# One skip op, tied weight loads, last value sums first, and three opening exps on VectorE in a fused attention and state-space kernel

**Chip, cores, metric.** One core of one Trainium2 chip. The metric is the device time of one execution in microseconds (us), lower is better. Each version was run several times; the rounds ran on different chips, each with runs of the kernel before beside the others. A stage's length is read from one profiled execution. The profile's span ends some 2 us before the reported time.

## The reference, cut to what matters

```python
def reference(A_x, A_Lambda_re, ..., B_wqkv, B_wo, gate_w):   # x: 1 x 2048 x 1024, bf16
    g = sigmoid((x * gate_w).sum(-1))
    # A: a state-space layer, h[t] = Lam_bar * h[t-1] + x[t] @ B_bar.T
    #    y = 2 * Re(h @ C.T) + x * Dskip                 <- the "skip"
    # B: attention, 32 heads of 32 columns, softmax over 2048 keys, then @ wo
    return g * a + (1 - g) * b
```

## The kernel before

The attention is cut into 512 bursts: TensorE (PE) makes the scores of four heads by 256 queries by 256 keys, ScalarE (ACT) or VectorE (DVE) takes the exponentials, PE multiplies with the values. The state-space work is woven in as dense chains of matmuls. The first 16 bursts are the opening: they run while the projections of the first heads are still being made and while GpSimd (POOL) makes the products from which the tables of the scan are built. ACT takes all exps of 128x1024, except that in the bursts of the set `DVB` VectorE takes half of one tile in four steps:

```python
def dve_exp(self, B, s, p):
    ...
    self.S.op("act", lambda e: e.activation(t[:, 0, :], ps[:, 2 * s, :], ACT.Exp, ...), ...)
    # exp_a: PSUM -> SBUF, frees the score bank when it is done
    self.S.op("dve", lambda e: e.tensor_scalar(xi, ps[:, 2 * s + 1, :], BITS_0, BITS_MIN, ALU.add, ALU.max), ...)
    # exp_b, exp_c, exp_d: each with two inputs in SBUF
    self.dx += [(0.603, lambda: self.dve(lambda e: e.scalar_tensor_tensor(xw, lo, 65536.0, lo, ALU.subtract, ALU.mult), ...)),
                (0.603, lambda: self.dve(lambda e: e.scalar_tensor_tensor(xw, lo, CUBE_C, xw, ALU.add, ALU.mult), ...)),
                (0.603, lambda: self.dve(lambda e: e.scalar_tensor_tensor(bits, xw, CUBE_K, xi, ALU.mult, ALU.add), ...)), ...]
```

POOL's products in the opening, 128x1024 f32, four multiplications and two additions:

```python
def products():
    for n, (u, v) in enumerate(((0, 0), (1, 1), (0, 1), (1, 0))):
        self.pool(lambda e, n=n, u=u, v=v: e.tensor_tensor(pr[n], hi[u], lo[v], ALU.mult), ...)
        if n % 2:
            ...
            self.pool(lambda e, ...: e.tensor_tensor(out, pr[n - 1], pr[n], ALU.add if r else ALU.subtract), ...)
```

The end of the last burst, and the end of each engine's stream, where a flag made from the row sums decides whether a safe second version must run (it never does here):

```python
        self.pv([(last - 1, q) for q in range(4)])
        preload()      # four matmuls, sum of the other heads' output
        pv(0)          # last value sums, 2 x 8 matmuls
        norm(0)
        pv(1)
...
            S.emit(name, e, sems, MARK_AT[name], lambda: loc.append(e.mark_branch_hint_location()))
            ...
            e.wait_ge(sems[fast.flag_op.lane], fast.flag_op.tick)
            with e.register("bad_" + name) as r:
                e.reg_load(r, flag[0:1, 0:1])
                br = e.br_cmp(r, 0, on_true="done_" + name, on_false="bad_" + name, comp_op="IS_EQ")
                ...                        # the second version stands between the branch and "done"
```

Of the kernel before, what the change touches and what calls it, by code (L numbers as in the profile page):

```python
# [735 lines left out]
class GpPhaseA:  # L736
# [216 lines left out]
ORDER = "".join(w[0] * int(w[1:]) for w in (  # L953
    "u2 p3 u2 p1 u3 p3 u1 p7 u3 p1 u3 p5 u1 p1 u5 p1 u1 p3 u2 p1 u1 c3 p1 c1 p2 u1 p1 u2 p1 c2 p1 c1 p1 u2 p1 u1 p1 u1 p3 c1 u3 p5 c1 u1 p1 u3 c1 p4 u2 p1 "
    "c1 u2 p1 c2 u2 p8 u2 p1 c1 p1 u2 p1 c5 p1 c5 u4 p3 u2 p4 u2 p1 u2 p1 u2 p3 u2 p3 u1 p2 u1 p5 c8 p2 o36 ").split())
DVB_RUNS = ((70, 70), (73, 73), (78, 82), (90, 94), (97, 97), (108, 108), (114, 114), (117, 117), (122, 122), (125, 125), (130, 130), (138, 142), (145, 149), (155, 155), (158, 158), (161, 161), (166, 166), (171, 171), (174, 174), (179, 179), (182, 214), (217, 217), (222, 226), (229, 229), (234, 250), (253, 253), (258, 262), (265, 265), (270, 274), (277, 277), (282, 290), (293, 305), (308, 308), (314, 318), (321, 321), (324, 324), (329, 329), (332, 332), (338, 342), (347, 347), (350, 354), (365, 365), (370, 370), (373, 373), (382, 382), (385, 389), (394, 394), (397, 397), (406, 410), (413, 417), (420, 420), (426, 426), (429, 429), (434, 438), (441, 445), (450, 450), (453, 453), (459, 459), (462, 470), (473, 481), (486, 490), (493, 497), (502, 506))
DVB = {B for lo, hi in DVB_RUNS for B in range(lo, hi + 1, 4)}
REST = 508
FIRST = 16
# [23 lines left out]
class FastPath:  # L983

    def __init__(self, nc, S, es, d, flag):
# [32 lines left out]
        self.prow = T("prow", [40, 128], BF)  # L1018
        self.pf = T("pf", [128, 40, 8], F32)
        self.W = T("W", [128, 2, 2, 8], F32)  # L1020
# [3 lines left out]
        self.drow = T("drow", [128, 1024], BF)  # L1024
        xa = T("xa", [128, 256], BF)
        self.init = T("init", [128, 2, 8], F32)
# [5 lines left out]
        self.badb = T("badb", [128, 2], BF)  # L1032
        self.xn = [xa[:], self.pf[:, 24:40, :].bitcast(BF).rearrange("p a b -> p (a b)")]

# [18 lines left out]
        self.xi = [wx[0][:, 2048:3072], wx[1][:, 2048:3072], self.ut[:, 0, :]]  # L1053
        self.xi = [ap.bitcast(F32) for ap in self.xi]
        self.xw = [ag, ag, self.ut[:, 1, :]]
        self.tile += self.xt
# [22 lines left out]
    def act(self, fn, r, w, name=""):  # L1079
        return self.S.op("act", fn, reads=r, writes=w, name=name)  # L1080

# [13 lines left out]
    def ld_w(self, g, part, eng="sp"):  # L1095
        cb = 1024 * part + 128 * g
        deps = []
        for t in self.x_toks(g % 2) if g > 2 else []:
            deps += [self.S.tok_w.get(t)] + list(self.S.tok_r.get(t, []))
        self.S.op(eng, lambda e: e.dma_start(self.w[:, g % 2, part], self.wsrc[:, :, cb:cb + 128]), writes=[("w", g % 2, part)], deps=deps, name="ld_w", dma=True)  # L1100
# [79 lines left out]
    def opening(self):  # L1180
# [12 lines left out]
        for word in self.OPENING.split():  # L1193
# [11 lines left out]
            elif op == "Kb":  # L1205
                self.half256(1, i, 1)
                evac(self.K[:, 0, 256 * i:256 * (i + 1)], 7, ("K", 0, i // 2), i % 2 == 0)
                self.spare(SPARE_K[i])
            elif op == "Qb":
                self.half256(0, i, 1)  # L1210
                evac(self.Q[:, i // 2, 256 * (i % 2):256 * (i % 2 + 1)], 7, ("Q", i // 2), i % 2 == 0)
                self.spare(SPARE_Q[i])
            elif op in ("Va", "Vb"):
# [8 lines left out]
                if h:  # L1222
                    src = ps[:, bank, 0:258].rearrange("p (k c) -> p k c", k=2)
                    S.op("dve", lambda e, i=i, src=src: e.tensor_copy(self.V[:, 0, 2 * i:2 * i + 2, :, 0:32], src[:, :, 0:128].rearrange("p k (h c) -> p k h c", h=4)),
                         reads=[("bank", bank)], name="evac_v", **(dict(acc=[("V", 0, i // 2)]) if i % 2 else dict(writes=[("V", 0, i // 2)])))
                    dve(lambda e, i=i, src=src: e.tensor_copy(self.gcol[:, 0, 2 * i:2 * i + 2], src[:, :, 128]), [("bank", bank)], [("g0", i)])
                    self.spare(SPARE_V[i])
            elif op == "G":
# [5 lines left out]
            elif op == "B":  # L1234
                self.burst(8 * U + i)()
                while self.later and self.later[0][0] <= self.p:
                    self.later.pop(0)[1]()
                self.p += 1
            elif op == "M":
                S.op("pe", lambda e: e.matmul(ps[:, 6, 0:40], self.prow[:], self.ident[0:40, 0:40], start=True, stop=True),  # L1240
                     reads=[("prm", i) for i in range(5)] + ["ident"], writes=[("bank", 6)], name="prm")
                dve(lambda e: e.tensor_copy(self.pf[:, 0:5, :], ps[:, 6, 0:40].rearrange("p (a b) -> p a b", a=5)), [("bank", 6)],
                    [("pf", i) for i in range(5)], "prm")
                dve(lambda e: e.tensor_copy(self.wv0[:, :, 128], self.pf[:, 4, :]), [("pf", 4)], ["wv0g"])
                self.bg2, self.bg3 = self.math()
                self.nmath = len(self.bg2)

    def spare(self, us):
# [102 lines left out]
    def ld_xn(self, ch, tq, cb):  # L1351

        tt = 4 * ch + tq
        for k in range(2):
            over = ["iot", "ioth", "ioti"] + [("pw2", l) for l in range(4)] if k and self.c_next == 0 else []
            c0 = 512 * cb + 256 * k
            self.dma(lambda e, k=k, c0=c0: e.dma_start(self.xn[k], self.x2[128 * tt:128 * (tt + 1), c0:c0 + 256]), [], [("xn", k)] + over, "ld_xn")
        self.c_next += 1

    def skip_ops(self, ch, tq, cb):  # L1360

        tt = 4 * ch + tq
        ops = []
        for k in range(2):
            c0 = 512 * cb + 256 * k
            ops.append((0.335, lambda k=k, c0=c0: self.dve(lambda e: e.scalar_tensor_tensor(self.Ag[:, 0, 256 * k:256 * (k + 1)], self.xn[k], self.gcol[:, 0, tt:tt + 1],
                                                                                            self.drow[:, c0:c0 + 256], ALU.mult, ALU.mult),
                                                           [("xn", k), "drow", "g0"], [("Ag", 0), ("sc", 0)] if k == 0 else [("Ag", 0, 1)], "skip")))
        ops.append((0.0, lambda: self.c_next < 32 and self.ld_xn(*self.c_list[self.c_next])))
        return ops  # L1370
# [16 lines left out]
    def table_ops(self, j):  # L1387
# [10 lines left out]
        def op(c, fn, r, w, *late):  # L1398
            ops.append((c, lambda: self.dve(fn, r, w)) + late)
        op(0.27, lambda e: e.tensor_scalar(S[:, :, 0:128], bj[:, :, 0:128], w(1, 0), None, ALU.mult), b0 + self.EFtok, [sc] + (["m_a0", "m_a1", "m_a2", "m_k", "m_h", "m_y"] if j == 0 else []))  # L1400
        for r, alu in ((0, ALU.subtract), (1, ALU.add)):
# [135 lines left out]
    def d_c(self, ch, tq, cb, k):  # L1537
# [15 lines left out]
        def evac():  # L1553
            self.dve(lambda e: e.scalar_tensor_tensor(a, ps[:, 7, :], self.gcol[:, 0, tt:tt + 1], a, ALU.mult, ALU.add), [("bank", 7), "g0", ("Ag", 0, 1)], [at], "evac_c")  # L1554
            self.dma(lambda e: e.dma_start(self.agd[tile], a), [at, ("Ag", 0, 1)], [("agd", tile)], "st_a")
            self.c_left[ch] -= 1
            self.c_end = self.p
# [172 lines left out]
    def x_set(self, B):  # L1730
        return 2 if B >= 433 else self.x_group(B) % 2

# [50 lines left out]
    def dve_exp(self, B, s, p):  # L1783
# [6 lines left out]
        wg = self.x_group(B)  # L1790
        use = (k, wg if k < 2 else 0)
        self.x_now = k
        if use not in self.seen_x:
            self.seen_x.add(use)
            if k < 2:
                assert self.busy_w != wg and not self.proj[wg]
                over = [("w", k, q) for q in range(3)] + [("Ag", 1), "m_h", "m_y"]
            else:
# [82 lines left out]
    def build(self):  # L1881
# [7 lines left out]
        self.dx, self.seen_x, self.waiting, self.x_now, self.busy_w = [], set(), set(), None, None  # L1889
        self.bg2, self.bg3 = [], []  # L1890
        self.begin()
# [53 lines left out]
        log = self.log = []  # L1945
        self.dx_end = {}
        for p in range(first, NBURST):
# [55 lines left out]
            if g + 2 < GROUPS:  # L2003
                assert g or pg != 24 or not (proj[0] or cur and cur.tag == "proj")
                for k, part in enumerate((1, 2, 0)):
                    if pg == (58 + 2 * k if g else 24):
                        self.ld_w(g + 2, part)
# [141 lines left out]
    def tail(self):  # L2149
# [61 lines left out]
        self.pv([(last - 1, q) for q in range(4)])  # L2211
        preload()
        pv(0)
        norm(0)
        pv(1)
        xp(0)
# [137 lines left out]
```

## Time and profile before

| | before |
|---|---|
| time, median of 3 runs | 918.78 us (918.45 to 919.16) |
| span of the profiled run | 916.8 us |
| first exp starts | 9.77 us |
| first normalization of a head ends the opening | 49.23 us |
| last full normalization | 899.32 us |
| flag write starts | 914.08 us |

The last four rows cut the span into five stages: **start** (to the first exp), **opening** (to the first 128x8 reciprocal of a normalization), **middle** (to the last such reciprocal), **tail** (to the flag) and **end**. The lines that show what bounds each stage stand in the prediction.

The end of the opening, its rows in the timeline (start, duration, engine, line, operation, output <- inputs):

```profile
39.55 0.17 DVE L1231 TENSOR_SCALAR f_gcol<-f_gcol 128x16 f32<-128x16 f32 x1 [0.86 <-ACT f_gcol L1230]
...
42.50 0.68 DVE L1523 CAST f_ub<-f_ps 128x512 bf16<-128x512 f32 x1
42.64 0.37 PE L1853 MATMUL f_ps<-f_V,f_OT 128*128 128x33 bf16 x8
...
43.32 1.02 PE L1517 MATMUL f_ps<-f_xT,f_wb 128*128 128x512 bf16 x4
```

At 39.55 VectorE waits 0.86 us for ACT, whose queue holds the sigmoid of the gate; then it makes the gate's column `gcol`, and from 40.13 the tables of the scan. The cast is the first evacuation (copy out of PSUM) of a chain `u`, the product of x with the input matrix of the state-space layer; it stands behind the tables in VectorE's queue. PE's next chain, which needs the bank, starts at 43.32.

### The profile page before, as it was taken

The numbers are of one execution on the slowest core, as the hardware profiler recorded it, in microseconds if no ns is written. First come the engines' busy times: TensorE is split into PE (matmuls) and PEld (weight loads), VectorE is DVE, ScalarE is ACT, GpSimd is POOL, SyncE is SP. The second block draws the span as 40 slices with busy tenths as digits, with TensorE's granted clock in tenths as the row PEclk, the third lists the DMA queues.
The fourth block names the chain that finished last, engine by engine and source line by source line (L and its number), as shares of the span: only waits on it lengthen the run. The fifth ranks groups of instructions, "written<-read, shape, count | busy, mean of one in ns | idle before, by whom it ended". The sixth has DMA issues, their size and how long they took to land.

```text
span 916.8 us, 33709 instructions
## 1 busy us (share of the span) xinstructions
PE 902.4 (98%) x15196; PEld 513.6 (56%) x15196; DVE 757.3 (83%) x1394; ACT 902.1 (98%) x1034; POOL 33.4 (4%) x63
## 2 busy tenths in 40 slices
PE   8999999999999999999999999999999999999997
PEld 4556655555555655665556555556555655555554
DVE  4499998999989899998988975789999776676675
ACT  6999999999999999999999999999999999999997
POOL 0500000010000001000000010000000000000000
PEclk9999999999999999999999999999999999999999
DMA  9558631322311305222222113231330122533422
GB/s 205 108 88 129 105 59 40 54 44 57 87 39 39 72 24 86 44 51 48 62 65 31 49 62 87 66 63 31 54 63 8 52 65 70 177 88 119 123 65 75
DMA packets 166867, 65.37 MB, mean 71 GB/s; under 512 B 146880, under 2 KB 155584, under 8 KB 166720
## 3 DMA queue, kind: packets, MB, share of 16 engines
q1 hardware_dynamic: 164416, 62.52, 30.8%
q8 instruction: 120, 1.97, 0.9%
q10 hardware_dynamic: 2304, 0.67, 0.3%
q14 instruction: 27, 0.22, 0.1%
HBM read 21.24 MB, written 12.62 MB: 37 GB/s over the span
## 4 chain that ended last, share of the span: by engine, by line
PE 92%; DVE 3%; ACT 3%; DMA 1%; issue 0%; SPq 0%
PE f_ps L1853 26%; PE f_ps L1758 18%; PE f_ps L1545 12%; PE f_ps L1517 12%; PE f_ps L1485 11%; PE f_ps L1578 6%; PE f_ps L1505 5%; ACT f_cT_re L1781 1%; DVE f_tq L1423 1%; ACT f_pt L1781 1%; DMA f_xT<-in_A_x_dram 1%; ACT f_cT_im L1781 1%; ACT f_Et L1781 1%; ACT f_OT L1781 1%; DVE f_ht L1431 1%
## 5 line engine op out<-in xcount | busy, mean ns | idle before, releaser
L1781 ACT ACTIVATE f_pt<-f_ps 128x1024 bf16<-128x1024 f32 x840 | 800.5, 1156 | 1.2 <-PE f_ps L1758 0.6
L1853 PEld LDWEIGHTS f_ps<-f_V,f_pt 128*128 128x128 bf16 x6720 | 232.8, 96 | 137.1 <-issue 86.5
L1853 PE MATMUL f_ps<-f_V,f_pt 128*128 128x33 bf16 x6720 | 285.4, 178 | 0.3
L1758 PE MATMUL f_ps<-f_Q,f_K 32*128 32x256 bf16 x4096 | 213.1, 273 | 2.6 <-ACT f_cT_re L1781 1.2
L1758 PEld LDWEIGHTS f_ps<-f_Q,f_K 32*128 32x128 bf16 x4096 | 67.4, 92 | 120.9 <-ACT f_pt L1781 63.4
L1517 PE MATMUL f_ps<-f_xT,f_wb 128*128 128x512 bf16 x512 | 131.1, 377 | 1.5 <-DVE f_ub L1523 0.4
L1485 PE MATMUL f_ps<-f_xT,f_wb 128*128 128x512 bf16 x464 | 119.0, 378 | 0.3 <-DVE f_Q L1490 0.2
L1431 DVE TENSOR_TENSOR_SCAN f_ht<-f_pf,f_init,f_ut 128x512 bf16<-128x512 f32 x64 | 81.2, 1275 | 0.0
L1805 DVE TENSOR_SCALAR f_wb<-f_ps 128x512 f32<-128x512 f32 x83 | 56.8, 685 | 27.4 <-PE f_ps L1758 26.5
L1545 PE MATMUL f_ps<-f_cT_re,f_hp 128*128 128x512 bf16 x192 | 72.6, 378 | 0.9 <-DVE f_Ag L1554 0.8
L1545 PE MATMUL f_ps<-f_cT_im,f_hp 128*128 128x512 bf16 x192 | 72.5, 378 | 0.0
L1578 PE MATMUL f_ps<-f_wb,f_OT 128*128 128x512 bf16 x248 | 63.9, 378 | 0.2
L1804 ACT ACTIVATE f_wb<-f_ps 128x512 bf16<-128x512 f32 x83 | 60.8, 732 | 0.6 <-PE f_ps L1758 0.6
L1517 PEld LDWEIGHTS f_ps<-f_xT,f_wb 128*128 128x128 bf16 x512 | 40.3, 96 | 34.2 <-issue 2.2
L1505 PE MATMUL f_ps<-f_wb,f_xT 128*128 128x128 bf16 x896 | 59.1, 219 | 0.3
L1812 DVE SCALAR_TENSOR_TENSOR f_wb<-f_Ag,f_wb 128x512 int16<-128x512 f32 x83 | 56.7, 683 | 0.6
L1811 DVE SCALAR_TENSOR_TENSOR f_Ag<-f_wb,f_Ag 128x512 f32<-128x512 uint16 x83 | 56.7, 683 | 0.5
L1810 DVE SCALAR_TENSOR_TENSOR f_Ag<-f_wb 128x512 f32<-128x512 uint16 x83 | 56.6, 682 | 0.3
L1485 PEld LDWEIGHTS f_ps<-f_xT,f_wb 128*128 128x128 bf16 x464 | 36.2, 96 | 28.7 <-DVE f_Q L1490 0.3
L1505 PEld LDWEIGHTS f_ps<-f_wb,f_xT 128*128 128x128 bf16 x896 | 50.5, 97 | 0.9 <-issue 0.4
L1523 DVE CAST f_ub<-f_ps 128x512 bf16<-128x512 f32 x48 | 33.1, 690 | 14.8 <-PE f_ps L1517 14.1
L1423 DVE TENSOR_TENSOR f_tq<-f_ht,f_Et 128x1024 bf16<-128x1024 bf16 x64 | 42.8, 685 | 0.4
(158 smaller groups left out, 892.7 us busy)
## 6 DMA issues: line engine op xcount, KB each, us to landing
ag_scratch<-f_Ag SPq DMA_DIRECT2D x32, 256.0 KB, 2.0
f_hp<-ag_scratch SPq DMA_DIRECT2D x32, 256.0 KB, 3.0
f_wb<-in_B_wqkv_dram SPq DMA_DIRECT2D x21, 256.0 KB, 4.0
out_dram<-f_xT SPq DMA_DIRECT2D x14, 256.0 KB, 2.1
f_xa<-in_A_x_dram SPq DMA_DIRECT2D x32, 64.0 KB, 1.9
f_pf<-in_A_x_dram SPq DMA_DIRECT2D x32, 64.0 KB, 1.9
f_wb<-in_B_wo_dram SPq DMA_DIRECT2D x1, 1024.0 KB
f_OT<-f_On SPq DMA_TRANSPOSE x63, 2.3
```

What stands on the lines that cost most here:

```text
L1431: ops.append((1.192, lambda ri=ri: dve(lambda e: e.tensor_tensor_scan(ht[:, ri, :], rr, ut[:, ri, :], self.init[:, ri, j:j + 1], ALU.mult, ...
L1485: mms.append((1, lambda e, f, l, a=a: e.matmul(ps[:, bank, :], w[:, g % 2, part, a, :], xT[:, a, 512 * ch:512 * (ch + 1)], start=f, stop=l ...
L1505: m = e.matmul(ps[:, bank, 128 * q:128 * (q + 1)], xT[:, a, 128 * kt:128 * (kt + 1)], w[:, g % 2, 2, a, :], start=(a == 0), stop=(a == 7))
L1517: mms.append((1, lambda e, f, l, a=a: e.matmul(ps[:, 7, :], bT[:, n % 2, ri, a, :], xT[:, a, 512 * ch:512 * (ch + 1)], start=f, stop=l), [ ...
L1545: mms.append((1, lambda e, f, l, j=j, ri=ri: e.matmul(ps[:, 7, :], hp(tq, ri, j), cT[ri][:, j, 512 * cb:512 * (cb + 1)], start=f, stop=l), ...
L1578: mms.append((1, lambda e, f, l, j=j: e.matmul(ps[:, 7, :], OT[:, j, 256 * qb + 128 * r:256 * qb + 128 * (r + 1)], wo[j][0][:, 512 * cb:51 ...
L1758: m = e.matmul(ps[:, 2 * sl[z] + h % 2, 256 * kl:256 * (kl + 1)], K[32 * h:32 * h + 32, g % 2, 128 * kt:128 * (kt + 1)], Q[32 * h:32 * h + ...
L1781: self.act(lambda e: e.activation(self.tile[p], ps[:, 2 * s:2 * s + 2, :], ACT.Exp, bias=OCTAVES * LN2, scale=LN2 / 128), [("S", s)], [("p ...
L1804: self.S.op("act", lambda e: e.activation(t[:, 0, :], ps[:, 2 * s, :], ACT.Exp, bias=OCTAVES * LN2, scale=LN2 / 128), reads=[("S", s)], wr ...
L1805: self.S.op("dve", lambda e: e.tensor_scalar(xi, ps[:, 2 * s + 1, :], BITS_0, BITS_MIN, ALU.add, ALU.max), reads=[("S", s)], writes=[("xi" ...
L1811: (0.603, lambda: self.dve(lambda e: e.scalar_tensor_tensor(xw, lo, CUBE_C, xw, ALU.add, ALU.mult), [I, W], [W], "exp_c")),
L1853: m = e.matmul(ps[:, 6, o:o + 33], self.tile[p][:, h2, 256 * kl + 128 * qt:256 * kl + 128 * (qt + 1)], V[:, g % 2, 2 * i + kl, h, :], star ...
```

## The change

The intent: give ACT less to do in the opening and at the very end, shorten the last serial chain, and use fewer, larger instructions for the skip. Weight loads are tied to an exp, and 24 tiny memsets, the pads, stand ahead of VectorE's stream; the record doesn't say what the pads are for. Core of the diff (cuts marked):

```diff
-DVB_RUNS = ((70, 70), (73, 73), ... (502, 506))
+DVB_RUNS = ((7, 7), (12, 12), (14, 14), (70, 70), (73, 73), ... (502, 506), (509, 509))
 ...                                   # and small exchanges in ORDER, the order of dense work
-        self.xi = [ap.bitcast(F32) for ap in self.xi]
+        self.xi = [ap.bitcast(F32) for ap in self.xi] + [self.Ag[:, 0, :]]   # scratch in the state bank
-        for k in range(2):            # x for the skip: two loads of 128x256
-            self.dma(... self.xn[k], self.x2[..., c0:c0 + 256] ...)
+        self.dma(... self.xn, self.x2[128 * tt:128 * (tt + 1), 512 * cb:512 * (cb + 1)] ...)
 ...                                   # one 128x512 skip op for two of 128x256
-        deps = []
-        for t in self.x_toks(g % 2) if g > 2 else []:
+        deps = [self.last_act] if g > 1 else []                              # tied weight loads
+        for t in self.x_toks(g % 2) if g > 1 else []:
+        for _ in range(24):
+            self.dve(lambda e: e.memset(self.chk[:, 5:6], 0.0), [], ["pad"])
-        preload()
         pv(0)
         norm(0)
+        preload()
         pv(1)
```

## The prediction

> **What bounds the kernel now.** I read the page first, then the stretches of five to ten microseconds, then the timeline of the first 56 and the last 20 us, last the chain of waits. The page's first part has two engines full at once and VectorE (DVE) behind them:
>
> ```profile
> PE 902.4 (98%) x15196; PEld 513.6 (56%) x15196; DVE 757.3 (83%) x1394; ACT 902.1 (98%) x1034; POOL 33.4 (4%) x63
> ```
>
> PE and ACT are both at 98%, so an average names no bound; it has to be found per stage. The stretches (columns: us, then busy time and count of PE, PEld, DVE, ACT, POOL, then clock, DMA share, GB/s) do that:
>
> ```profile
> 25.00:30.00 5.00, 4.81 (x66) 3.24 (x64) 2.86 (x10) 5.00 (x6) 3.76 (x2) 1.00 1.16 175
> 30.00:35.00 5.00, 4.18 (x61) 2.94 (x60) 1.41 (x5) 5.00 (x7) 4.92 (x4) 1.00 0.80 173
> 35.00:40.00 5.00, 4.62 (x77) 3.08 (x72) 1.40 (x6) 5.00 (x7) 3.64 (x2) 1.00 0.02 5
> 50.00:60.00 10.00, 10.00 (x197) 5.73 (x190) 9.91 (x18) 10.00 (x12) 0.71 (x1) 1.00 0.53 89
> ```
>
> In the opening (16 bursts, first exp at 9.77 us, last ends near 41 us) ACT is never idle, while PE has gaps and DVE is two thirds idle from 30 to 40 us: ACT bounds it. From 50 us on PE and ACT are both full, and until 100 us DVE too. Note POOL: it is at work from 26 to 39 us and nearly nowhere else. The last burst is a serial chain of PE, DVE and ACT.
>
> [...]
>
> ```profile
> 190.95 2.12 POOL L1456 TENSOR_TENSOR f_cm<-f_hl,f_W 128x8 f32<-128x8 f32 x4
> 191.12 0.68 DVE L1812 SCALAR_TENSOR_TENSOR f_wb<-f_Ag,f_wb 128x512 int16<-128x512 f32 x1
> 191.72 1.30 DVE L1423 TENSOR_TENSOR f_tq<-f_ht,f_Et 128x1024 bf16<-128x1024 bf16 x2
> ...
> 362.06 0.68 POOL L1456 TENSOR_TENSOR f_cm<-f_hl,f_W 128x8 f32<-128x8 f32 x4
> ```
>
> The same four POOL products take 0.68 us where DVE reads PSUM, and 2.12 us beside two-input DVE instructions, whose own length stays at 0.68. Here POOL waits, not DVE; a long POOL instruction against DVE is not in this trace. [...] The twelve warm-up matmuls take 4.46 us in the trace, the first ones 0.43 us apart[...]. [...]
>
> **The change, part by part.**
>
> *Three exps of the opening.* Bursts 7, 12 and 14 run as the 11th, 13th and 15th. ACT drops one 128x1024 exp in each to 128x512. Full exps: the 11th burst's starts at 28.22 us and the 16th's at 37.25, so ten take 9.03 us, 0.903 each. Half an exp is seen at the end (start, duration, engine):
>
> ```profile
> 898.71 0.79 ACT L1804 ACTIVATE f_ub<-f_ps 128x512 bf16<-128x512 f32 x1
> ...
> 899.18 8.56 ACT L1781 ACTIVATE f_pt<-f_ps 128x1024 bf16<-128x1024 f32 x9
> ```
>
> The next starts 0.47 us on. Saved: 0.903 - 0.47 = 0.43 each, 1.3 us for three. DVE gets four 128x512 instructions each at about 0.6 us start to start, 3 x 2.4 = 7.3 us, from 28 to 40 us, where its idle time is about 7 us: it fits just, and the evacuations slip by less than one burst.
>
> *One more at burst 509.* The ACT row above is back to back up to the last exp, so ACT bounds the last bursts too; a gain of up to 0.43, call it 0.35, as PE has only some 0.3 us of wait a burst there.
>
> *Last value sums first.* The end of the chain before:
>
> ```profile
> 909.01 0.55 PEld L2162 LDWEIGHTS f_ps<-f_Et,f_ident 128*128 128x128 bf16 x4
> 909.04 1.02 PE L2162 MATMUL f_ps<-f_Et,f_ident 128*128 128x512 bf16 x4
> 909.68 0.47 PEld L2173 LDWEIGHTS f_ps<-f_V,f_pt 128*128 128x128 bf16 x8
> 909.90 0.36 PE L2173 MATMUL f_ps<-f_V,f_pt 128*128 128x33 bf16 x8
> 910.29 0.18 DVE L2180 RECIPROCAL f_rc<-f_ps 128x4 f32<-128x4 f32 x1 [0.91 <-PE f_ps L2173]
> ```
>
> Four preload matmuls stand ahead of the eight value sums that the reciprocal waits for. Exchanged, the sums start at about 909.1, the reciprocal near 909.55, and the preload fills PE while DVE normalizes (0.76 us of PE wait there before). The second sums then wait for the preload's end, near 910.3 instead of 911.02. Gain about 0.7.
>
> *24 pads.* The new DVE program starts with 24 one-column memsets, each waiting for the one before, ahead of the memset that releases the warm-up. The warm-up before ends at 5.71 us (1.25 + 4.46), the first projection starts at 6.67, when its transposed load has landed; 0.96 us is free. A DVE accumulator read (one column) takes 0.08 us, so I estimate 0.08 per pad, 1.9 us in all: the projection starts near 7.6, 0.95 late. A second load wait of 0.16 us is absorbed: cost 0.8 us, moved straight into the first exp, as nothing in the opening has slack on ACT. At 0.04 us a pad it would be nothing, at 0.12 it would be 1.8.
>
> *Skip op, weight loads, order of work.* Two 128x256 skip instructions start 0.39 us apart, 0.79 a pair; one of 512 columns should take about 0.66 (256 more columns at 0.96 per ns). 32 x 0.13 = 4 us of DVE, in a stage where DVE has idle time: 0 on the path. One 128 KB load for two of 64 KB: hidden. Group 2's weights come 34 bursts later and all others are tied to an exp; they land within 4 us and are first needed about six bursts on, some 10 us: 0. Two small exchanges in the order of dense work: 0, give or take 0.5.
>
> *Sum without a new wait:* -1.3 - 0.35 - 0.7 + 0.8 = -1.55, or 917.2 us.
>
> **The rivals.** (1) *POOL's products become the wait.* The tables' first DVE instruction needs POOL's last product:
>
> ```profile
> 36.36 2.36 POOL L1323 TENSOR_TENSOR f_OT<-f_hp 128x1024 f32<-128x1024 f32 x1
> ...
> 40.13 0.35 DVE L1400 TENSOR_SCALAR f_Ag<-f_OT,f_rc 128x256 f32<-128x256 f32 x1
> ```
>
> POOL ends at 38.72, DVE comes at 40.13: 1.4 us of slack, which a shorter opening uses up. POOL reads SBUF all the while, and of the nine new two-input DVE instructions (three per exp) about eight fall beside it. If each holds POOL off for 0.53 us (512 columns at 0.96 per ns), POOL ends 4 us later, and DVE, which works in order, stands before the tables for some 3 us with the first u evacuation behind them; PE's next chain needs that bank, and PE works in order too. That would swallow the opening's gain and add about 3 us: 920 to 922. For it speaks the pair of POOL rows above; against it, that these were tiny instructions[...]. If instead the long POOL instruction (1.9 to 2.4 us) holds DVE off, exp_a of the next burst comes late, score banks stay taken and ACT stalls: 923 to 925. Against that: no two-input DVE row in the trace is longer than its kind. (2) *The pads dominate:* 0.12 us each gives +1.8, about 918.3. (3) *Nothing carries:* PE takes over as the bound in the last six opening bursts (it is busy 4.2 to 4.8 of 5 us) and only half of 1.3 us is seen: 917.9.
>
> I give the case without a new wait six in ten, the POOL wait three, DVE held off by POOL one. That weights the point by +0.4: 917.6 us. The range takes half of the POOL cases: 915.5 to 921.3. A gain of 2% would be 18 us; everything touched is below 10 us, so faster 0.01, same 0.98, slower 0.01.
>
> **What would show it.** Right: the first exp at about 10.6 us instead of 9.77, ACT without gap until the 16th burst's end near 40.4, three 128x512 exps there, POOL's end before 40 us, the first sums' reciprocal less than 0.6 us after the last score matmuls' sums, and 50 to 890 us as long as before. Wrong: POOL products longer than 1.91 and 2.36 us, a DVE wait of microseconds ahead of the tables, with PE idle near 44 us; or a first projection at 6.7 us (pads free) or after 8.5 (pads dear). If the middle stage (100 to 890 us) moves by more than 1 us, the order of work mattered, and my zero there is the failed step.

Two things that the prediction uses are seen in the traces with these numbers. The column rate: in the kernel before, VectorE's casts out of PSUM took 690 ns for 128x512 and 424 for 128x256, so 256 more columns took 266 ns, 0.96 per ns; the 0.66 us for a skip op and the 0.53 us for 512 columns are my estimates from this rate. The order of work: VectorE stood idle from 38.69 to 39.55 for ACT, and the tables behind, whose last POOL product had ended at 38.72, began only at 40.13; in only_15 (below) PE stood 1.83 us before a chain `u` and took the next scores after it, at 47.16, while ACT waited 1.43 us for them.

## The result and the profile after

The changed kernel takes **930.04 us** (median of 5, 929.2 to 930.48), the kernel before 918.88 in the same rounds (918.45 to 919.49). The ratio is 1.0119, 95% interval 1.0104 to 1.0134. Here and below a ratio is the record's, taken over fast runs of the same rounds, so not quite the ratio of the medians quoted. It is within 2%, as predicted, but the time lies 8.7 us above the range. The result is correct.

By stages, from the two profiled runs:

| | start | opening | middle | tail | end | sum |
|---|---|---|---|---|---|---|
| after minus before, us | +1.26 | **+7.27** | +0.36 | +0.03 | **+2.00** | +10.92 |
| predicted, before the weighting for the rivals | +0.8 | -1.3 | 0 | -0.35 - 0.7 | 0 | -1.55 |

The page's first part answers to the line shown before:

```profile
PE 884.8 (95%) x14977; PEld 515.1 (56%) x15196; DVE 771.1 (83%) x1402; ACT 901.4 (97%) x1034; POOL 36.5 (4%) x63
```

Nothing alarming: ACT has a little less to do, POOL 3 us more. (PE's lower figure tells little: 219 of its matmuls have no record in this trace, 14977 in place of 15196.) The loss is only to be seen by stretches (columns: us, then busy time and count of PE, PEld, DVE, ACT, POOL, then clock, DMA share, GB/s):

```profile
30.00:35.00 5.00, 3.47 (x47) 2.30 (x44) 5.00 (x8) 4.37 (x6) 4.92 (x3) 1.00 1.16 216
35.00:40.00 5.00, 3.02 (x33) 1.65 (x33) 4.76 (x8) 1.69 (x2) 4.92 (x3) 0.76 0.07 11
40.00:50.00 10.00, 8.32 (x95) 5.44 (x97) 8.10 (x19) 6.71 (x10) 1.52 (x1) 0.61 0.01 2
50.00:60.00 10.00, 9.09 (x174) 5.34 (x175) 7.03 (x19) 9.47 (x11) 0.00 (x0) 1.00 0.30 62
```

Where ACT was full before, it now works 1.69 of 5 us, while VectorE is full from 30 us, and it is full with only 8 instructions in 5 us, which is long for 128x512. From 35 us on the clock column falls as well, to 0.61, after PE's gaps (3.47 and 3.02 us busy of 5); that they cause it was not tested. The timeline of the changed kernel shows the instructions (POOL's rows with x2 are two in a row; the brackets at the end give the idle time before, and who ended it):

```profile
27.50 3.82 POOL L1331 TENSOR_TENSOR f_hp<-f_rc 128x1024 f32<-128x1024 f32 x2 [24.58 <-DVE f_rc L1322]
...
30.23 1.64 DVE L1819 SCALAR_TENSOR_TENSOR f_Ag<-f_Ag 128x512 f32<-128x512 uint16 x1
...
31.41 2.69 POOL L1335 TENSOR_TENSOR f_OT<-f_hp 128x1024 f32<-128x1024 f32 x1
32.13 2.51 DVE L1820 SCALAR_TENSOR_TENSOR f_Ag<-f_Ag 128x512 f32<-128x512 uint16 x1
...
34.04 4.73 POOL L1331 TENSOR_TENSOR f_hp<-f_rc 128x1024 f32<-128x1024 f32 x2
34.90 0.14 DVE L1229 COPY f_gcol<-f_ps 128x2 f32<-128x2 f32 x1
34.97 2.01 DVE L1821 SCALAR_TENSOR_TENSOR f_cT_re<-f_Ag 128x512 int16<-128x512 f32 x1
35.10 0.64 PE L1222 MATMUL f_ps<-f_OT,f_xT 128*128 128x129 bf16 x8 [1.62 <-DVE f_gcol L1229]
37.08 0.69 DVE L1814 TENSOR_SCALAR f_Ag<-f_ps 128x512 f32<-128x512 f32 x1
37.83 0.60 PE L1765 MATMUL f_ps<-f_Q,f_K 32*128 32x256 bf16 x6 [1.88 <-DVE f_Ag L1814]
38.02 1.29 DVE L1819 SCALAR_TENSOR_TENSOR f_Ag<-f_Ag 128x512 f32<-128x512 uint16 x1
38.31 1.02 ACT L1788 ACTIVATE f_cT_re<-f_ps 128x1024 bf16<-128x1024 f32 x1 [3.94 <-PE f_ps L1765]
38.85 2.68 POOL L1335 TENSOR_TENSOR f_OT<-f_hp 128x1024 f32<-128x1024 f32 x1
...
39.86 2.22 DVE L1820 SCALAR_TENSOR_TENSOR f_Ag<-f_Ag 128x512 f32<-128x512 uint16 x1
...
42.11 0.69 DVE L1821 SCALAR_TENSOR_TENSOR f_cT_re<-f_Ag 128x512 int16<-128x512 f32 x1
```

Read the ends. Five two-input steps run while POOL is at work; their lengths are 1.64, 2.51, 2.01, 1.29 and 2.22 us, where the sixth, after POOL's end, has its ordinary 0.69. The first ends at 31.87, the POOL pair at 31.32: 0.55 later. The second ends at 34.64, POOL's addition at 34.10: 0.54 later. The trace's single records of POOL (its instructions end at 36.43, 38.77 and 41.53) give 0.55, 0.54 and 0.55 for the other three. So each step waits until the POOL instruction that was under way has ended, and then does its work in a fixed time. The other way round, a POOL instruction that comes up while such a step does its work is later too: the second pair takes 4.73 in place of 3.82, the additions 2.69 and 2.68 in place of 2.36. exp_a (L1814), which reads PSUM, keeps its 0.69 beside POOL. The five waits add up to 9.67 - 5 x 0.68 = 6.27 us of VectorE.

From there the path is short. The evacuation of gcol stands in VectorE's queue behind the second step, which ended at 34.64; it starts at 34.90 and is late (PE idle 1.62 us), and so is the next burst's exp_a, which holds score banks (PE idle 1.88 us before scores); ACT then waits 3.94 us for scores.

### The profile page after: what moved, and what is told of

Read it like the earlier page. It is cut to its first block, busy times and chain, and to the rows that moved or that the text cites. A ratio compares the mean times of both kernels' runs of the same rounds, so it can differ in the third digit from the quotient of the medians.

```text
span 927.8 us, 33466 instructions
## 1 busy us (share of the span) xinstructions
PE 884.8 (95%) x14977; PEld 515.1 (56%) x15196; DVE 771.1 (83%) x1402; ACT 901.4 (97%) x1034; POOL 36.5 (4%) x63
## 4 chain that ended last, share of the span: by engine, by line
PE 80%; ACT 10%; DVE 6%; issue 2%; DMA 1%; DVEq 0%
PE f_ps L1862 23%; PE f_ps L1765 16%; PE f_ps L1552 11%; PE f_ps L1524 10%; PE f_ps L1492 9%; ACT f_pt L1788 8%; PE f_ps L1512 5%; PE f_ps L1585 4%; DMA ag_scratch<-f_Ag 1%; ACT f_OT L1788 1%; DVE f_Ag L1820 1%; ACT f_Et L1788 1%; DVE f_tq L1430 1%; PE f_ps L1148 0%; DVE f_ht L1438 0%
## 5 line engine op out<-in xcount | busy, mean ns | idle before, releaser
L1524 PE MATMUL f_ps<-f_xT,f_wb 128*128 128x512 bf16 x448 | 118.5, 378 | 9.2 <-issue 3.2
L1492 PE MATMUL f_ps<-f_xT,f_wb 128*128 128x512 bf16 x406 | 106.8, 378 | 5.6 <-issue 0.9
L1438 DVE TENSOR_TENSOR_SCAN f_ht<-f_pfx,f_init,f_ut 128x512 bf16<-128x512 f32 x64 | 81.2, 1275 | 0.0
L1814 DVE TENSOR_SCALAR f_wb<-f_ps 128x512 f32<-128x512 f32 x83 | 56.8, 685 | 27.3 <-PE f_ps L1765 26.0
L1552 PE MATMUL f_ps<-f_cT_im,f_hp 128*128 128x512 bf16 x180 | 68.0, 378 | 3.4 <-DVE f_Ag L1561 1.2
L1552 PE MATMUL f_ps<-f_cT_re,f_hp 128*128 128x512 bf16 x157 | 59.4, 378 | 0.8
L1585 PE MATMUL f_ps<-f_wb,f_OT 128*128 128x512 bf16 x217 | 57.5, 378 | 2.7 <-issue 0.2
```

What stands on the lines that cost most here:

```text
L1438: ops.append((1.192, lambda ri=ri: dve(lambda e: e.tensor_tensor_scan(ht[:, ri, :], rr, ut[:, ri, :], self.init[:, ri, j:j + 1], ALU.mult, ...
L1492: mms.append((1, lambda e, f, l, a=a: e.matmul(ps[:, bank, :], w[:, g % 2, part, a, :], xT[:, a, 512 * ch:512 * (ch + 1)], start=f, stop=l ...
L1524: mms.append((1, lambda e, f, l, a=a: e.matmul(ps[:, 7, :], bT[:, n % 2, ri, a, :], xT[:, a, 512 * ch:512 * (ch + 1)], start=f, stop=l), [ ...
L1552: mms.append((1, lambda e, f, l, j=j, ri=ri: e.matmul(ps[:, 7, :], hp(tq, ri, j), cT[ri][:, j, 512 * cb:512 * (cb + 1)], start=f, stop=l), ...
L1585: mms.append((1, lambda e, f, l, j=j: e.matmul(ps[:, 7, :], OT[:, j, 256 * qb + 128 * r:256 * qb + 128 * (r + 1)], wo[j][0][:, 512 * cb:51 ...
```

## The experiments

Twelve variants, each taken from the changed kernel unless it is said otherwise. This table holds the stages of all (profiled run minus that of the kernel before, us), and the times. The kernel before had medians of 918.72 (no_open to only_15), 918.86 (sp_nops to best) and 918.88 (the last four) beside them.

| kernel | start | opening | middle | tail | end | time us (range), ratio |
|---|---|---|---|---|---|---|
| no_open | +1.79 | +0.13 | +0.10 | +0.04 | +2.00 | 923.25 (922.1 to 924.04), 1.0052 |
| pool_fill | +2.14 | +0.35 | +0.40 | +0.04 | +1.31 | 922.49 (921.89 to 924.95), 1.0048 |
| no_pads | +0.28 | +7.40 | -0.18 | +0.04 | +1.26 | 927.21 (926.99 to 929.49), 1.0101 |
| only_15 | +1.57 | +1.31 | -0.07 | +0.04 | +1.35 | 923.05 (922.68 to 923.27), 1.0049 |
| sp_nops | +1.78 | +6.38 | -0.21 | +0.04 | +1.61 | 928.57 (928.29 to 929.75), 1.0110 |
| no_509 | +2.84 | +7.33 | -0.07 | -0.86 | +1.35 | 928.49 (927.01 to 929.51), 1.0101 |
| no_swap | +2.73 | +7.28 | +0.63 | +1.09 | +1.12 | 930.97 (930.77 to 931.43), 1.0131 |
| best | +0.01 | +0.32 | +0.15 | -0.86 | +1.49 | 919.70 (919.26 to 920.38), 1.0010 |
| sp_waits | +1.28 | +6.82 | -0.22 | +0.04 | 0.00 | 927.60 (926.57 to 929.0), 1.0100 |
| best_waits | -0.03 | +0.14 | 0.00 | -0.86 | 0.00 | 917.98 (917.83 to 918.88), 0.9993 |
| swap_only | +0.13 | +0.27 | -0.44 | -0.86 | -0.01 | 917.73 (917.61 to 917.87), 0.9988 |
| one_fill | -0.06 | -0.25 | -0.37 | +0.04 | +1.39 | 919.61 (919.44 to 919.94), 1.0009 |

**What the table can resolve.** The tail repeats to 0.01 us. The start repeats only where there are no pads. An opening without the exps comes out between +0.13 and +0.32, and the middle scatters by some 0.5 us; smaller things there are not to be told from one profile.

### The opening: no_open, pool_fill, no_pads

Two theories of the loss stood before these runs: VectorE's exp steps are held off by POOL's reads, or VectorE simply has too much to do. In the expectations of pool_fill and only_15 the first outcome is that of the first theory. no_open takes the three exps out:

```diff
-DVB_RUNS = ((7, 7), (12, 12), (14, 14), (70, 70), ...
+DVB_RUNS = ((70, 70), ...
```

> The changed kernel with bursts 7, 12 and 14 left wholly to ScalarE; pads, skip op, burst 509 and the exchange stay. Both theories of the opening[...] put the 7.3 us that the first normalization lost beyond the later start on these three exps: that normalization's reciprocal should come at 49.2 + 1.3 = 50.5 us, and the run at about 930.0 - 7.3 = 922.7 us. If it stays above 927 the loss is elsewhere in the opening.

pool_fill keeps them, and makes POOL's six products into fills of the same size, which write and read nothing. The result is wrong (relative error 0.031).

```diff
-self.pool(lambda e, n=n, u=u, v=v: e.tensor_tensor(pr[n], hi[u], lo[v], ALU.mult), ...)
+self.pool(lambda e, n=n, u=u, v=v: e.memset(pr[n], 0.0), ...)
-self.pool(lambda e, ...: e.tensor_tensor(out, pr[n - 1], pr[n], ALU.add if r else ALU.subtract), ...)
+self.pool(lambda e, ...: e.memset(out, 0.0), ...)
```

> The changed kernel with GpSimd's six products replaced by memsets of the same tiles: GpSimd still writes, but reads no SBUF (the tables are zero, so the result is wrong on purpose). [...] VectorE's two-input exp steps fall from 1.3-2.5 us to 0.7, PE and ScalarE no longer stall, the first normalization comes near 49.2 + 1.3 - 1.3 = 49.2 us, up to 49.8, and the run takes about 930.0 - 8.3 = 921.7 us. VectorE overloaded: nothing changes, normalization at 57 us, 929 to 930 us.

Without the exps the loss of 7.27 us is gone, so they cause it. With them, and with a POOL that only writes, it is gone as well. Its timeline:

```profile
31.11 0.68 DVE L1819 SCALAR_TENSOR_TENSOR f_Ag<-f_Ag 128x512 f32<-128x512 uint16 x1
31.16 1.85 POOL L1331 MEMSET f_hp<- 128x1024 f32 x2
...
32.05 0.68 DVE L1820 SCALAR_TENSOR_TENSOR f_Ag<-f_Ag 128x512 f32<-128x512 uint16 x1
...
33.06 0.95 POOL L1335 MEMSET f_OT<- 128x1024 f32 x1
...
33.36 0.68 DVE L1821 SCALAR_TENSOR_TENSOR f_cT_re<-f_Ag 128x512 int16<-128x512 f32 x1
```

All nine steps take 0.68 or 0.69 us, those beside a fill too. This separates the two rivals: VectorE was not simply given too much work, it was held off by POOL's reads. (The fills are also shorter than the products, 0.95 against 1.9 us; but the three steps above lie beside them.)

no_pads (the loop of 24 made 0) keeps the exps and POOL's products:

```diff
-        for _ in range(24):
+        for _ in range(0):
```

> The changed kernel without the 24 memsets. They took 2.95 us in the trace and moved the first exp from 9.77 to 11.03 us. If that is all they do: first exp at 9.8 us, 930.0 - 1.3 = 928.8 us. If they pay for themselves by where VectorE's instructions come to lie, the time stays at 930 or rises.

The opening loses 7.40 us again: the loss does not depend on the pads. The start is 1.0 us shorter than in the changed kernel. The time lies 1.6 us under the expected 928.8, since the end (+1.26 in place of +2.00) and the middle came out shorter too.

### Where the gain of the exps went: only_15 and one_fill

pool_fill has no collision and yet shows none of the predicted 1.3 us. only_15 puts just one exp on VectorE, in burst 15, the last of the opening, when POOL is done; the result is correct.

```diff
-DVB_RUNS = ((7, 7), (12, 12), (14, 14), (70, 70), ...
+DVB_RUNS = ((15, 15), (70, 70), ...
```

> The changed kernel with burst 15 (the 16th of the opening) on VectorE in place of 7, 12 and 14: its two-input steps come when GpSimd's products are over or nearly so. [...] the steps take 0.7 us each, the first normalization near 50.2 us (one exp saved against 50.5), about 922.3 us. VectorE overloaded: a third of the load costs about a third of 7.3 us, normalization near 53 us, about 925 us.

This expectation fell. The steps take 0.68 us, but the opening is 1.31 us longer. Its timeline at the end of the opening:

```profile
40.18 0.68 DVE L1819 SCALAR_TENSOR_TENSOR f_Ag<-f_Ag 128x512 f32<-128x512 uint16 x1
...
42.07 0.69 DVE L1821 SCALAR_TENSOR_TENSOR f_cT_re<-f_Ag 128x512 int16<-128x512 f32 x1
...
42.87 0.35 DVE L1407 TENSOR_SCALAR f_Ag<-f_OT,f_rc 128x256 f32<-128x256 f32 x1
...
45.37 0.68 DVE L1530 CAST f_ub<-f_ps 128x512 bf16<-128x512 f32 x1
46.42 0.81 PE L1524 MATMUL f_ps<-f_xT,f_wb 128*128 128x512 bf16 x3 [1.83 <-DVE f_ub L1530]
```

The exp's steps stand ahead of the tables (L1407 and on), the tables ahead of the cast that frees PE's bank, and PE waits 1.83 us for it. My new theory was: this queue of VectorE, not ACT, sets the end of the opening. one_fill was to test it: fills on POOL as in pool_fill, no pads, and only burst 7's exp on VectorE, the earliest, whose steps end well ahead of the tables (wrong result, as above).

```diff
-DVB_RUNS = ((7, 7), (12, 12), (14, 14), (70, 70), ...
+DVB_RUNS = ((7, 7), (70, 70), ...
```

> Wrong result on purpose: the six long GpSimd products are fills that only write, no pads, and of the three opening exps only burst 7's stays on VectorE, the first of them, whose four steps end some 7 us before the tables begin. Theory Q (without collisions the exps still gain nothing because VectorE's queue of steps, tables and the u evacuation sets the end of the opening): with the one early exp VectorE reaches the tables no later than before, so the opening from first exp to first normalization is 0.2 to 0.4 us shorter than in the kernel before. Rival (a burst's half exp on ScalarE is no gain in any case, because TensorE sets the pace from about 34 us on): the opening is as long as before, within 0.15.

The opening is 0.25 us shorter than before, the only one that is shorter. The fairer comparison is with the changed kernel without opening exps (no_open, best, best_waits: +0.13 to +0.32): against no_open the one early exp gains 0.38 us, and 0.43 was predicted for one. No run has the fills and no exps. The theory holds only in part, for in one_fill VectorE waits for ACT ahead of the tables, as in the kernel before:

```profile
39.11 0.17 DVE L1235 TENSOR_SCALAR f_gcol<-f_gcol 128x16 f32<-128x16 f32 x1 [0.86 <-ACT f_gcol L1234]
```

So in these two kernels, where no step of an exp stands right ahead of the tables, ACT sets when they begin. In pool_fill and only_15 ACT comes to the sigmoid of the gate earlier than in no_open as well, by 0.45 and 0.34 us counted from the first exp, but steps stand ahead of the tables, and these begin 0.21 and 1.17 us later than in no_open. The start of the first u cast, counted from the first exp, shows where the difference arises:

| | first exp | first u cast | between | minus before | opening minus before |
|---|---|---|---|---|---|
| before | 9.77 | 42.50 | 32.73 | | |
| one_fill | 9.71 | 42.18 | 32.47 | -0.26 | -0.25 |
| no_open | 11.56 | 44.41 | 32.85 | +0.12 | +0.13 |
| pool_fill | 11.91 | 44.98 | 33.07 | +0.34 | +0.35 |
| only_15 | 11.34 | 45.37 | 34.03 | +1.30 | +1.31 |
| after | 11.03 | 51.02 | 39.99 | +7.26 | +7.27 |

All of the opening's difference has arisen by the time VectorE makes this cast. So an exp in the opening gains when its steps end ahead of the tables, and costs when they come late. The gain is one profile's reading, 0.25 or 0.38 us by what it is compared with, close to the scatter; the losses of 1.31 and 7.27 are not. What two or three early exps would gain was not run.

### The tail: no_509 and no_swap

```diff
 # no_509
-..., (502, 506), (509, 509))
+..., (502, 506))
 # no_swap
+        preload()
         pv(0)
         norm(0)
-        preload()
         pv(1)
```

> The changed kernel without burst 509's exp on VectorE; the exchanged order of the tail stays. Theory T (tail: the exchange is worth 0.7 us, and burst 509 takes it back, since TensorE waits for VectorE's exp of it): from the last full normalization to the flag 0.5 to 0.7 us less than the changed kernel, about 929.4. Rival (509 gains what was predicted, and the exchange gives nothing): 0.35 us more, about 930.4.

> The changed kernel with the old order of the tail (preload matmuls ahead of the last value sums), burst 509's exp still on VectorE. Theory T: from the last full normalization to the flag 0.6 to 0.8 us more than the changed kernel, about 930.7. Rival (the exchange gives nothing): unchanged, 930.0.

The tail of the changed kernel was as long as before, +0.03. Without burst 509's exp it is 0.86 shorter than before; without the exchange 1.09 longer. So the exchange gains 0.86 to 1.06 (0.6 to 0.8 were expected), and burst 509 costs 0.89 us. Why it costs is in the timeline of the changed kernel:

```profile
916.06 0.74 DVE L1591 SCALAR_TENSOR_TENSOR f_xT<-f_ps,f_gcol,f_xT 128x512 bf16<-128x512 f32 x1
...
916.72 0.68 DVE L1821 SCALAR_TENSOR_TENSOR f_ub<-f_ut 128x512 int16<-128x512 f32 x1
917.46 0.27 PE L1862 MATMUL f_ps<-f_V,f_ub 128*128 128x33 bf16 x4 [1.22 <-DVE f_ub L1821]
```

PE's value sums wait 1.22 us for the last exp step, which stands behind an output evacuation in VectorE's queue; no later burst is left to fill PE. In no_509 the same place goes on without that wait, and the exchange does what was predicted, the sums ahead of the preload matmuls, which now run beside VectorE's normalization:

```profile
919.14 0.35 PE L2183 MATMUL f_ps<-f_V,f_pt 128*128 128x33 bf16 x8
919.34 1.02 PE L2172 MATMUL f_ps<-f_Et,f_ident 128*128 128x512 bf16 x4
919.53 0.18 DVE L2190 RECIPROCAL f_rc<-f_ps 128x4 f32<-128x4 f32 x1
...
920.26 0.35 PE L2183 MATMUL f_ps<-f_V,f_pt 128*128 128x33 bf16 x8
```

### The end: best, sp_nops, sp_waits, best_waits

best takes out all that had shown a cost (opening exps, pads, burst 509), and keeps the single skip op, tied loads, order of work and exchange.

> The changed kernel without the three opening exps, without the 24 pads and without burst 509: what stays is one skip op, the tied weight loads, the exchanges in the order of work and the tail's exchange. If the four costs found so far are all there is (opening 7.1, pads 1.0 to 1.5, burst 509 0.6, SyncE's branch), only the branch's 1.3 to 2.0 us and the tail's gain of 0.7 are left over the kernel before: 919.3 to 920.2. Under 918.5 would mean that the branch's extra time is not tied to SyncE's shorter stream; over 921 that there is another cost in the middle stage.

It came out at 919.70, inside the expected 919.3 to 920.2. What is left over the kernel before is the end: +1.49 us. SyncE closes with a conditional branch. This is from the trace's records of SyncE and of its instruction fetch packets (us; the fetch is counted from the branch):

```
             branch at   next event   gap    instruction fetch that starts at the branch
before        915.76      916.29      0.53   none within 0.4 us
after         924.77      927.20      2.44   at +0.07, takes 0.74
best          915.46      917.40      1.94   at +0.01, takes 0.53
sp_nops       923.84      925.89      2.05   at +0.10, takes 0.45
sp_waits      923.68      924.21      0.53   none within 0.4 us
best_waits    915.01      915.54      0.53   none within 0.4 us
```

Merging the x loads for the skip took 32 loads and six waits out of SyncE's stream: as built it has 603 instructions in place of 641, so the branch and its target stand 38 places earlier. My theory was that this place decides whether the target has to be fetched. The trace has 32 fewer loads and six fewer waits, too. sp_nops was to put the place back with no-operations:

```diff
+            if eng_name == "sp" and mark is not None and k == 150:
+                for _ in range(58):
+                    eng.nop()
```

> The changed kernel with 58 no-operations in the middle of SyncE's stream, in place of the 58 instructions (32 loads with their waits) that merging the x loads took out, so that SyncE's closing branch stands where it did before the change. Theory P (position of the branch in the stream decides an instruction fetch): the branch-to-next-event time falls from 2.44 us to about 0.5, and the kernel takes 1.3 to 2.0 us less than the changed one: about 928.3. Rival (the end grew for another reason, for example the longer VectorE program): the branch still takes 1.7 us or more, and the time stays at 930. The opening's loss of 7 us is untouched in both.

Nothing changed at the branch, but this run tested nothing: the 58 bare no-operations are not in the built stream, which still has 603 instructions. Nor was 58, a count of operations with their waits, the right number. (Its opening, +6.38, and that of sp_waits, +6.82, are shorter. The traces show this much: in the changed kernel and the five variants with the three exps and POOL's products, the five steps are held off for 6.3 to 6.5 us. By the trace's clock records the clock then stood at half for 10.2 us or more in four of the six, but for two stretches of 3.4 us in these two.) sp_waits uses waits on a value that has been reached long before, 38 of them; the built stream has 641 instructions with them:

```diff
-                eng.wait_ge(sems[l], t * (16 if l.startswith("dma") else 1))
+                for _ in range(39 if eng_name == "sp" and mark is not None and k in (150, 151) and l == o.waits[0][0] else 1):
+                    eng.wait_ge(sems[l], t * (16 if l.startswith("dma") else 1))
```

> The changed kernel with 38 more waits in the middle of SyncE's stream, on a semaphore value that is reached already, so that its closing branch stands at the same place of the built stream as before the change (the built stream has 641 instructions before, 603 after, 641 in this one; the no-operations of the earlier try were dropped by the build, which so tested nothing). Theory P: the branch takes about 0.5 us in place of 1.6 to 2.4, the end is 1.1 to 1.9 us shorter, the kernel near 928.3. Rival: branch unchanged at 1.6 to 2.4 us, time 929.5 to 930.

best_waits is best with the same waits.

> The changed kernel without opening exps, pads and burst 509, and with the same 38 waits in SyncE's stream. Theory P: 919.7 of the kernel without these waits falls by 1.1 to 1.5 us, to 918.3 (0.6 under the kernel before, as the tail's exchange gains 0.86 and the opening loses 0.3). Rival: 919.7 again.

In both the stream has 641 instructions again, the gap is 0.53 us to the hundredth, no fetch starts at the branch, and the end is as long as before. best falls by 1.72 us to 917.98 by getting 38 useless waits (in other rounds; the kernel before took 918.86 and 918.88 beside them). In the table a fetch starts at the branch in the three traces with the short stream and in none of the three with the long one. That the length of SyncE's stream decides is shown by the waits; that the fetch is the cost is not: the fetch at the branch takes 0.45 to 0.74 us, the gap 1.94 to 2.44, and what fills the rest stays open.

### The exchange alone: swap_only

The kernel before with one edit, the exchange of the tail (as in the diff of the change); its SyncE stream keeps its 641 instructions.

> The kernel before with one part of the change alone: the last value sums ahead of the preload matmuls. SyncE's stream has its old length of 641. Theory T and P together: tail 0.86 to 1.06 shorter, opening, middle and end as before: 917.9 to 918.1 against 918.85. If the branch at the end takes 1.5 us or more here too, theory P falls and the time is 919 or more.

917.73 us, 1.1 below the kernel before. The ranges of the runs do not touch (917.61 to 917.87 against 918.32 to 919.2), though the interval of the ratio just reaches 1 (0.9974 to 1.0001). In the profile the tail gives -0.86 of the difference of -0.91.

## Why the prediction was wrong

**The opening exps, predicted -1.3, measured +7.27.** Two steps failed. The first is the wait: "Here POOL waits, not DVE". In the changed kernel VectorE waited for POOL, five steps for 6.27 us together, and without POOL's reads (pool_fill) the loss was gone. The second is the overlap: "it fits just, and the evacuations slip by less than one burst". Even without collisions steps of the exps stood ahead of the tables, and PE waited for the u cast, 1.11 us in pool_fill and 1.83 in only_15. That ACT bounds the opening holds up to the tables; one early exp gained 0.38 us against no_open. That nothing behind had room could have been read in the trace of before: the u cast ended 0.14 us before PE's chain started.

The rivals were weighted the wrong way round. The prediction had the collision with the right consequence (exp_a late, score banks taken, ACT stalled), but gave "DVE held off by POOL one" chance in ten, at 923 to 925. Its evidence was four tiny POOL products, 2.12 us together, beside which VectorE's two-input steps kept their 0.68 us. Its argument against, that no two-input VectorE row was longer than its kind, could not count: beside the six long POOL instructions of that trace there is none. POOL was busy 12.3 of the 15 us from 25 to 40, and in the five us from 30 it was busy 4.92: a VectorE step that comes at a random moment finds it at work. An estimate from the prediction's own rows, 1.91 and 2.36 us for one POOL instruction: half of one, about 1.0 us, for each step beside POOL, so five steps make 5 us; measured were 6.27. (The prediction counted about eight of the nine steps beside POOL.) The weighting has an error of its own, too: six tenths of 917.2, three of about 921 and one of 924 make 919.0, so +1.8 and not +0.4. The wait for POOL is shown by pool_fill (0.68 or 0.69 us a step without its reads); how the 6.27 us of VectorE become 7.27 us of path, with the clock at 0.61 after PE's gaps, was only read from the trace.

**The pads, predicted +0.8, measured +1.26** in the changed kernel, and +1.28 to +2.84 in the other variants with pads. The first sign is the length of a pad:

```profile
0.87 2.95 DVE L1901 MEMSET f_chk<- 128x1 f32 x24 [0.87 <-PEq L2349]
...
4.15 4.09 PE L1148 MATMUL f_ps<-f_hp 128*128 128x512 bf16 x12 [4.15 <-DVE f_hp L1120]
```

24 memsets take 2.95 us, 0.123 each, not 0.08: the prediction's own "at 0.12 it would be 1.8" is near the mean of the eight profiles with pads (1.92). The term was mis-sized: it took a busy time, the 0.08 us of an accumulator read, where the distance from start to start counts. A pad is busy 0.059 us, and the next starts 0.126 us after it. The scatter comes from the warm-up behind them. Before, the warm-up has 0.95 us to spare until the load lands; now the projection waits for it, and its twelve matmuls took 4.09 us here and 5.30 in no_509:

```profile
4.14 5.30 PE L1148 MATMUL f_ps<-f_hp 128*128 128x512 bf16 x12 [4.14 <-DVE f_hp L1120]
...
9.24 2.38 PE L1166 MATMUL f_ps<-f_xT,f_wb 128*128 128x128 bf16 x32
```

There even the projection takes 2.38 us in place of 1.95. The traces' clock records show why: the matmuls start 0.43 us apart until the full clock is granted and 0.22 after, and it was granted at 6.88 us here and at 10.12 in no_509. In the eight profiles with pads the later it was granted, the later the first exp. Counted from the first warm-up matmul it came after 2.7 to 6.0 us in all the profiles. So the small +1.26 is in part luck. What sets the moment stays open.

**Last value sums first, predicted -0.7, measured -0.86.** Right, reciprocal and preload as drawn; a little mis-sized.

**Burst 509, predicted -0.35, measured +0.89.** The step that failed: the row of ACT back to back was read as ACT bounding the last bursts. What ACT saves there ends as waiting, because PE needs VectorE's half of that burst and has nothing else left to do.

**The end, predicted 0, measured +2.00** (1.1 to 2.0 in all variants with the short stream). "One 128 KB load for two of 64 KB: hidden" was right of the data; the number of SyncE's instructions was not looked at.

**Skip op, weight loads, order of work, predicted 0.** Right within the scatter: best_waits keeps all of them and has a middle stage of +-0.00 and an opening of +0.14. A skip instruction takes 745 ns for two of 477: 268 ns for 256 more columns, 0.96 per ns, as the prediction had it.

Checked by its sum: the changed kernel's +7.27, +2.00, +1.26, +0.36 and +0.03 make 10.92 us, the whole difference of the spans.

## What to carry to other kernels

Before you move work to VectorE beside GpSimd, look at how long each GpSimd instruction is and how much of that stretch is filled with them: here a two-input VectorE instruction from SBUF waited for the end of whichever GpSimd instruction with inputs from SBUF was under way (five steps ended 0.54 to 0.55 us after it, and took 1.29 to 2.51 us in place of 0.68), and everything behind it in its queue waited too. A bound that holds "through a stage" need not hold at its end: find the instruction that releases the next stage, and see how much slack it has. With 38 instructions fewer on SyncE the gap after its closing branch grew here from 0.53 us to between 1.94 and 2.44, so compare this gap before and after.
